# A two-layer network behind attention: the second layer in three groups of 768 tokens, its first product by seven block products, its weights decoded in batches 1 to 3

## The chip, the cores and the metric

The kernel runs on one core of a Trainium2 chip. The metric is the device time of one execution in microseconds (us), the median of three runs; lower is better. A core has TensorE (PE, matrix products into PSUM), VectorE (DVE), ScalarE (ACT), GpSimd (POOL) and SyncE (SP, which here issues every DMA, in order).

## The reference, cut to what matters

Four batches of 576 tokens (2304 in all) pass through an attention with 8 heads of 64, a gated layer, and a plain layer with SiLU:

```python
x = attention(q, k, v, s)                    # 2304 x 512
g = x @ w_gate; v = x @ w_val                # 512 -> 1536
x = (silu(g) * v) @ w_out                    # 1536 -> 512   (first layer)
h = x @ w_in                                 # 512 -> 2048
out = silu(h) @ w_out2                       # 2048 -> 512   (second layer)
```

All is float32. The weights arrive as 64-bit words and are decoded in the kernel.

## The kernel before, in words

**Products in three parts.** A matmul input is split into a rounded high part and the remainder (`hi` by an ACT copy, `lo` by a subtraction on POOL or DVE). Each product of 128 x 128 weights is three matmuls into the same PSUM bank: high x high, high x low, low x high (`mm3`, L432 to L434). Everything is held transposed: 128 features on the partitions, tokens along the free dimension.

**Decode.** A piece of weights is 512 words per partition (512 KB, tile `r64`). `decode` makes 512 float32 values of it with two ACT instructions (L392, L393) and two on DVE (L394, L397). `w_cut` then makes the high and low halves, 1024 columns at a time, on ACT (L101) and on POOL or DVE (L410).

**First layer.** Each batch runs nine chunks of 2048 weight columns, in the order of `L1`: six for gate and value, three for the way down. A chunk is 96 matmuls of 288 columns. In batch 0 its weights are decoded and also stored as float32 in DRAM (`w32`); batches 1 to 3 load them from there. While batch b runs its chunks, the attention of batch b + 1 is worked on between their steps. Batch 3 has no attention beside it. Its last chunks split the first weights of the second layer. The results go to DRAM (`x2_d`, L477).

**Second layer.** `stream` has eight chunks `uo`, each with 256 hidden features: their columns of `w_in` and their rows of `w_out2`. A chunk's weights are loaded as 64-bit words, decoded and split once. For each chunk the five token blocks of `TB` pass (four of 464 tokens, one of 448). `up2` makes two tiles of 128 hidden features with 12 matmuls each, and `silu_mul` turns them into split tiles: tanh on ACT (L441), multiply on DVE (L443), high part on ACT (L101), low part on POOL (L447). `down2` of the block before makes four output tiles with six matmuls each, and adds them into accumulators in SBUF (L525 on ACT in the first chunk, L527 on DVE after it). The split tokens (`x2_in`: load, ACT copy, DVE subtraction at L500) are made once and stay in SBUF.

**Order.** Up to the end of batch 0's attention the order of all engines is the program's. From then to the start of batch 3 PE's order is the program's and a planner with a timeline of its own orders the other engines. From batch 3 on (`manual.close()`, L644) it orders PE too. The planner may run an instruction well ahead of its place in the program where its inputs and its buffer are there. Within an engine, and within SP's DMA queue, the order is then fixed.

**Buffers.** Tiles of one tag share a fixed number of buffers in turn: five `wraw` buffers hold raw words, decoded values and loaded float32 weights; four each of `wh` and `wl` hold split weights; `ps_m` is four PSUM banks and `ps_o` four more in the second layer. A new tile waits until the earlier tile in its place is released.

## Time and profile before

| | |
|---|---|
| median of 3 runs | 1086.63 us (1085.73 to 1088.04) |
| profiled execution | 1088.26 us, span 1086.3 us |
| PE / DVE / ACT / POOL busy | 96% / 54% / 48% / 42% of the span |
| DMA | 111.90 MB, mean 103 GB/s |

The time of a run holds a little more than the span, which reaches from the first to the last recorded instruction. Busy times of different engines overlap. A matmul's recorded duration is longer than the distance to the next one, since they are pipelined; what a matmul costs is read from the distance of the starts.

### The profile page before, as it was taken

To read this page: it belongs to the slowest core of one execution; us is meant where nothing else is said; L and a number is where in the kernel's file an instruction comes from. 1 tells how busy PE (TensorE), PEld (TensorE's weight loads), DVE (VectorE), ACT (ScalarE), POOL (GpSimd) and SP (SyncE) were. 2 spreads that over 40 slices of the span, in tenths; PEclk is the share of its full clock that TensorE was granted. 3 is DMA by queue.
4 is the path that set the end of the run, shared out by engine and by line. 5 is a ranking of instruction groups with operands and counts; after the bars stand their busy time and mean duration, and the time that the engine had idled before them with its cause. 6 is when DMAs were issued, how large, how long until landed. Compare 5 with 4: busy or idle time off the path is not lost. (4 is left out here: it accounts for less than half of the span.)

```text
span 1086.3 us, 18550 instructions
## 1 busy us (share of the span) xinstructions
PE 1048.2 (96%) x6768; PEld 942.5 (87%) x6768; DVE 590.2 (54%) x1411; ACT 522.2 (48%) x1134; POOL 451.5 (42%) x587
## 2 busy tenths in 40 slices
PE   8779899999999999999989999999999999999998
PEld 5448789899998999898989999898989898898887
DVE  5668677846555646636554347615464554643333
ACT  6667776745655435655444435744243343322221
POOL 4555655554646346546315343332322232332221
PEclk8789999999999999999999999999999999999999
DMA  8556686573343334212163224601010111000012
GB/s 230 137 171 202 203 219 220 167 223 113 79 133 94 117 110 122 89 40 90 40 188 114 81 78 142 204 20 59 20 59 20 59 39 40 20 1 1 1 63 112
DMA packets 46699, 111.90 MB, mean 103 GB/s; under 512 B 7249, under 2 KB 20561, under 8 KB 46609
## 3 DMA queue, kind: packets, MB, share of 16 engines
q1 hardware_dynamic: 46608, 110.73, 33.1%
q8 instruction: 53, 0.87, 0.3%
q14 instruction: 38, 0.30, 0.1%
HBM read 91.76 MB, written 18.95 MB: 102 GB/s over the span
## 5 line engine op out<-in xcount | busy, mean ns | idle before, releaser
L447 POOL TENSOR_TENSOR h<-u,h 128x288 fp32r<-128x288 f32 (+2 forms) x176 | 195.2, 1111 | 355.8 <-ACT h L101 353.1
L432 PE MATMUL po<-h,wh 128*128 128x288 f32 (+2 forms) x704 | 233.1, 332 | 3.2 <-DVE xt L327 2.0
L432 PE MATMUL pgv<-xt,wh 128*128 128x288 f32 x768 | 229.6, 299 | 3.2 <-DVE u L443 2.0
L433 PE MATMUL po<-h,wh 128*128 128x288 f32 (+2 forms) x704 | 231.9, 329 | 0.1
L434 PE MATMUL po<-h,wl 128*128 128x288 f32 (+2 forms) x704 | 230.9, 328 | 0.0
L434 PE MATMUL pgv<-xt,wl 128*128 128x288 f32 x768 | 226.1, 294 | 0.0
L433 PE MATMUL pgv<-xt,wh 128*128 128x288 f32 x768 | 226.1, 294 | 0.0
L410 POOL TENSOR_TENSOR wl<-wraw,wh 128x1024 fp32r<-128x1024 f32 x53 | 126.6, 2390 | 158.1 <-ACT wh L101 136.1
L432 PEld LDWEIGHTS pgv<-xt,wh 128*128 128x128 f32 x768 | 144.0, 188 | 14.7 <-DVE m L218 4.5
L101 ACT ACTIVATE h<-u 128x288 fp32r<-128x288 f32 (+2 forms) x176 | 89.3, 508 | 120.4 <-DVE u L445 69.1
L432 PEld LDWEIGHTS po<-h,wh 128*128 128x128 f32 x704 | 131.9, 188 | 14.9 <-DVE m L218 2.3
L433 PEld LDWEIGHTS pgv<-xt,wh 128*128 128x128 f32 x768 | 144.2, 188 | 0.0
L434 PEld LDWEIGHTS pgv<-xt,wl 128*128 128x128 f32 x768 | 144.1, 188 | 0.0
L434 PEld LDWEIGHTS po<-h,wl 128*128 128x128 f32 x704 | 132.1, 188 | 6.9
L433 PEld LDWEIGHTS po<-h,wh 128*128 128x128 f32 x704 | 132.1, 188 | 6.8 <-POOL h L447 0.5
L443 DVE SCALAR_TENSOR_TENSOR u<-th,pu 128x464 f32<-128x464 f32 (+1 forms) x80 | 50.6, 633 | 138.3 <-ACT th L441 138.3
L527 DVE SCALAR_TENSOR_TENSOR acc<-po,acc 128x464 f32<-128x464 f32 (+1 forms) x140 | 88.4, 635 | 62.3 <-PE po L434 61.7
L101 ACT ACTIVATE wh<-wraw 128x1024 fp32r<-128x1024 f32 x88 | 92.0, 1056 | 57.6 <-PE po L433 41.8
L433 PE MATMUL pu<-x,wh 128*128 128x464 f32 (+1 forms) x320 | 118.9, 371 | 0.0
L432 PE MATMUL pu<-x,wh 128*128 128x464 f32 (+1 forms) x320 | 118.5, 370 | 0.0
L434 PE MATMUL pu<-x,wl 128*128 128x464 f32 (+1 forms) x320 | 118.5, 370 | 0.0
L231 ACT ACTIVATE e<-e,m 64x64 f32<-64x64 f32 (+4 forms) x160 | 88.6, 555 | 60.2 <-DVE m L218 59.5
(63 smaller groups left out, 1451.0 us busy)
## 6 DMA issues: line engine op xcount, KB each, us to landing
wraw<-w SPq DMA_DIRECT2D x54, 512.0 KB, 4.6
r<-in_w_dram SPq DMA_DIRECT2D x52, 512.0 KB, 6.2
qkr<-in_qk_dram SPq DMA_DIRECT2D x32, 288.0 KB, 7.4
w<-wraw SPq DMA_DIRECT2D x18, 512.0 KB, 4.0
cumb<-cum_d SPq DMA_DIRECT2D x15, 576.0 KB, 7.8
r<-in_w_dram SPq DMA_DIRECT2D x32, 256.0 KB, 3.1
x_d<-acc SPq DMA_DIRECT2D x32, 144.0 KB, 2.7
vrb<-in_vb_dram SPq DMA_DIRECT2D x16, 256.0 KB, 3.0
```

The source lines that it names most:

```text
L101: nc.scalar.activation(out=out, in_=in_, func=AF.Copy, scale=scale)
L231: nc.scalar.activation(out=e[:r, hd, :wd], in_=e[:r, hd, :wd], func=AF.Exp, bias=m[hd][:r], scale=-1.0, accum_out=l[:r, hd : hd + 1],)
L410: engines[WL[phase[c]][e]].tensor_tensor(out=wl, in0=t, in1=wh.bitcast(F32), op=ALU.subtract)
L432: nc.tensor.matmul(out=ps[:, :n], lhsT=a, rhs=xh, start=(k == 0), stop=False)
L433: nc.tensor.matmul(out=ps[:, :n], lhsT=a, rhs=xl, start=False, stop=False)
L434: nc.tensor.matmul(out=ps[:, :n], lhsT=c, rhs=xh, start=False, stop=(k == last))
L443: nc.vector.scalar_tensor_tensor(out=u, in0=th[:, :n], scalar=1.0, in1=pg[:, :n], op0=ALU.add, op1=ALU.mult)
L447: engines[LO[ph]].tensor_tensor(out=lo, in0=u, in1=hi.bitcast(F32), op=ALU.subtract)
L527: nc.vector.scalar_tensor_tensor(out=a, in0=ps[:, :n], scalar=0.5, in1=a, op0=ALU.mult, op1=ALU.add)
```

## The change

The second layer no longer takes the tokens in five blocks for every weight chunk. It runs three groups of 768 tokens (`TG`), each in two halves of 384 (`TN`), and within a group eight steps of 256 hidden features (`steps`, 24 in all).

The first product of a step is a 2 x 2 block product (halves of the 512 inputs x halves of the 256 features, against halves of the inputs x halves of the 768 tokens). It is done with seven block products in place of eight, on sums and differences of blocks (`UP`). A block product is six matmuls of 384 columns. A step's weights lie in three tiles: Z holds the three plain weight blocks that are used (768 columns), S four sums and differences of blocks, D the rows of `w_out2`. Two banks take two products each, with an ACT copy of the first one between (`s0`, `s4`); a third takes two with a copy as well (`s1`). The four results are put together on DVE and POOL, and each goes through `silu2`.

The 32 pieces of the second layer's weights are decoded in batches 1 to 3 (`ahead_load`, `ahead`) and stored as float32 in `w32`. In group 0 they are loaded, combined and split (`u_load`, `u_cut`), and the split tiles are stored in `wu_d`. Groups 1 and 2 load the split tiles. The tokens of a group are loaded and combined into seven split tiles (`x2_load`, `x2_first`, `x2_rest`), the next group's during step 7 of this one. PE keeps the program's order to the end. Split weights of the first layer now lie in one tile `wt` (high and low half).

```diff
-NCH = NGV + NO1 + NU + NO2
+NGV, NO1, NU, NO2, NPR = 6, 3, 4, 4, 8
+TG, TN = 3, 384
+UP = [("Z", 0, 0, "a"), ("S", 0, 1, "d"), ("Z", 1, 2, "a"), ("S", 1, 3, "b"), ("S", 2, 4, "c"), ("S", 3, 5, "d"), ("Z", 2, 6, "c")]
...
+    def ahead_load(i):
+        p, e = divmod(i, CW // DW)
+        t = wst["r", i] = raw_p.tile([P, DW, 2], U32, tag="wraw", name="r64")
...
+    def ahead(i):
+        p, e = divmod(i, CW // DW)
+        z = raw_p.tile([P, CW // 2], F32, tag="wraw", name="z32")
+        unpack(z[:, :DW], wst.pop(("r", i)), dec_p.tile([P, DW], U32, tag="dk", name="dk"))
+        nc.sync.dma_start(out=w32[len(L1) + p, :, e * DW : (e + 1) * DW], in_=z[:, :DW])
...
+    def x2_first(t):
+        u, d = p2["x2", 0], p2["x2", 1]
+        x2_cut(t, 0, u[:, :, 0])
+        t1 = p2["t1"] = x2_sub(t, u[:, :, 1], u[:, :, 0])
+        x2_cut(t, 1, t1)
+        x2_cut(t, 2, d[:, :, 0])
+
+    def x2_rest(t):
+        u, d = p2["x2", 0], p2["x2", 1]
+        t2 = x2_sub(t, d[:, :, 1], p2["t1"])
+        x2_cut(t, 3, t2)
+        x2_cut(t, 4, x2_sub(t, d[:, :, 1], u[:, :, 1]))
+        x2_cut(t, 5, d[:, :, 1])
+        x2_cut(t, 6, x2_sub(t, d[:, :, 0], t2))
...
+    def u_load(i):
+        t, p = steps[i]
+        for k, name in enumerate("ZSD"):
+            wide = 768 if name == "Z" else CW // 2
+            if t > 0:
+                w = p2["w", i, name] = u_tile()
+                nc.sync.dma_start(out=w[:, :, :wide].bitcast(F32), in_=wu_d[p, k, :, :, :wide])
+            elif name != "S":
+                r = p2["r", i, name] = stage(CW // 2)
...
+    def u_cut(i, names="ZSD"):
...
+                for o, a, b, op in (
+                    (s1, a21, a22, ALU.add), (s2, s1, a11, ALU.subtract),
+                    (s3, a11, a21, ALU.subtract), (s4, a12, s2, ALU.subtract),
+                ):
+                    nc.vector.tensor_tensor(out=o, in0=a, in1=b, op=op)
...
+            copy("a", hi, r[:, :wide])
+            eng = nc.vector if name == "D" else nc.gpsimd
+            eng.tensor_tensor(out=lo, in0=r[:, :wide], in1=hi.bitcast(F32), op=ALU.subtract)
+            nc.sync.dma_start(out=wu_d[p, "ZSD".index(name), :, :, :wide], in_=w[:, :, :wide].bitcast(F32))
...
+    def silu2(hi, lo, src):
+        th = p2["tmp"].tile([P, TN], F32, tag="th", name="th")
+        u = p2["tmp"].tile([P, TN], F32, tag="u", name="u")
+        nc.scalar.activation(out=th, in_=src, func=AF.Tanh, scale=0.5)
+        nc.vector.scalar_tensor_tensor(out=u, in0=th, scalar=1.0, in1=src, op0=ALU.add, op1=ALU.mult)
+        copy("a", hi, u)
+        nc.gpsimd.tensor_tensor(out=lo, in0=u, in1=hi.bitcast(F32), op=ALU.subtract)
+
+    def up2(i):
...
+        for name, k, xi, bank in UP:
+            w, x = p2["w", i, name], p2["x", t, xi]
+            fresh = bank not in ps
+            if fresh:
+                ps[bank] = ps_m.tile([P, 512], F32, tag="m", name="pu")
+            o = ps[bank][:, :TN]
+            for kk in range(2):
+                c0 = k * 256 + kk * P
+                a, c = w[:, 0, c0 : c0 + P], w[:, 1, c0 : c0 + P]
+                nc.tensor.matmul(out=o, lhsT=a, rhs=x[:, 0, kk], start=fresh and kk == 0, stop=False, skip_group_check=True)
+                nc.tensor.matmul(out=o, lhsT=a, rhs=x[:, 1, kk], start=False, stop=False, skip_group_check=True)
+                nc.tensor.matmul(out=o, lhsT=c, rhs=x[:, 0, kk], start=False, stop=kk == 1, skip_group_check=True)
+            if xi in (0, 1, 4):
+                nc.scalar.activation(out=part(f"s{xi}"), in_=o, func=AF.Copy)
+            if xi == 2:
+                silu2(h[0][0][:, 0], h[0][0][:, 1], o)
+            if xi == 3:
+                nc.vector.tensor_tensor(out=part("u2"), in0=o, in1=tmp["s0"], op=ALU.add)
+            if xi == 4:
+                nc.gpsimd.tensor_tensor(out=tmp["s1"], in0=tmp["s1"], in1=tmp["s4"], op=ALU.add)
+                nc.gpsimd.tensor_tensor(out=tmp["s1"], in0=tmp["s1"], in1=tmp["u2"], op=ALU.add)
+            if xi == 5:
+                nc.vector.tensor_tensor(out=part("c12"), in0=o, in1=tmp["u2"], op=ALU.add)
+                silu2(h[0][1][:, 0], h[0][1][:, 1], tmp["c12"])
+                silu2(h[1][1][:, 0], h[1][1][:, 1], tmp["s1"])
+            if xi == 6:
+                nc.vector.tensor_tensor(out=part("c21"), in0=o, in1=tmp["u2"], op=ALU.add)
+                silu2(h[1][0][:, 0], h[1][0][:, 1], tmp["c21"])
...
-        manual = ExitStack()
-        manual.enter_context(tc.manual_schedule(engines={mybir.EngineType.PE}))
+        everything.enter_context(tc.manual_schedule(engines={mybir.EngineType.PE}))
+        later = [[] for _ in range(n1)]
+        for i in range(NPR * CW // DW):
+            later[len(L1) + i if i < 18 else 3 * len(L1) + (i - 18) // 2].append(i)
...
-                manual.close()
+                p2["x2"] = pool("x2", 10, scope=second_layer, side="right")
...
+                if n == 0 and c == n1 - 1:
+                    u_load(0)
+                    u_cut(0)
...
+        p2["wt2"] = pool("wt2", 4, scope=second_layer)
+        p2["st"] = pool("st", 4, scope=second_layer)
+        p2["tmp"] = pool("tmp2", 1, scope=second_layer)
+        p2["h"] = pool("h2", 8, scope=second_layer)
+        u_load(1)
+        for i, (t, p) in enumerate(steps):
+            if i + 1 < len(steps):
+                u_cut(i + 1)
+            if i + 2 < len(steps):
+                u_load(i + 2)
+            if t + 1 < TG and p == 3:
+                x2_load(t + 1)
+            if t + 1 < TG and p == NPR - 1:
+                x2_first(t + 1)
+            up2(i)
+            if t + 1 < TG and p == NPR - 1:
+                x2_rest(t + 1)
+            if i > 0:
+                down2(i - 1)
+        down2(len(steps) - 1)
```

`down2(i)` is as before in kind: for each half of 384 tokens and each of four output tiles, six matmuls into a `ps_o` bank, then one instruction of 384 columns into the accumulator (ACT in step 0 of a group, DVE after it).

## Rows read from the trace of the kernel before

**Rows 1.** The page, part 1: busy us (share of the span) xinstructions.

```profile
PE 1048.2 (96%) x6768; PEld 942.5 (87%) x6768; DVE 590.2 (54%) x1411; ACT 522.2 (48%) x1134; POOL 451.5 (42%) x587
```

**Rows 2.** The page, part 4: the chain by engine, shares of the span.

```profile
PE 36%; DVE 1%; DMA 1%; issue 1%; ACT 1%; SPq 0%; DVEq 0%; ACTq 0%
```

**Rows 3.** Timeline of PE: start us, us, engine, line, operation, tile.

```profile
571.44 0.40 PE L432 MATMUL pgv<-xt,wh 128*128 128x288 f32 x1 [2.00 <-DVE u L443]
...
679.66 0.38 PE L432 MATMUL pu<-x,wh 128*128 128x464 f32 x1
```

**Rows 4.** The second layer's stretch: length, busy us by engine, PE clock, DMA share, GB/s.

```profile
679.66:1082.38 402.72, 401.40 (x1922) 359.84 (x1920) 188.22 (x283) 144.47 (x250) 114.54 (x87) 1.00 0.14 47
```

**Rows 5.** The chain in order of time: start us, us, what.

```profile
978.36 0.22 PE pu L434
...
1028.45 0.22 PE pu L434
```

**Rows 6.** Groups by form: busy us, mean ns of one, idle before.

```profile
L101 ACT ACTIVATE wh<-wraw 128x1024 fp32r<-128x1024 f32 x88 | 92.0, 1056 | 57.6 <-PE po L433 41.8 <-PE pgv L433 13.4 <-PE pu L433 1.7
...
L397 DVE SCALAR_TENSOR_TENSOR wraw<-r,dk 128x512 uint32<-128x512 uint32 x68 | 53.8, 800 | 0.6
...
L394 DVE SCALAR_TENSOR_TENSOR dk<-wraw,dk 128x512 uint32<-128x512 uint32 x68 | 50.7, 760 | 10.9 <-ACT dk L393 6.8 <-ACT wraw L392 3.7
...
L393 ACT ACTIVATE dk<-r 128x512 uint32<-128x512 uint32 x68 | 44.1, 650 | 35.4 <-DMA r<-in_w_dram 27.9 <-DVE u L443 3.0 <-DVE wraw L397 2.4
...
L392 ACT ACTIVATE wraw<-r 128x512 f32<-128x512 f32 x68 | 43.9, 667 | 21.8 <-DVE wl L410 7.6 <-DMA w<-wraw 4.8 <-issue 3.2
...
L443 DVE SCALAR_TENSOR_TENSOR u<-th,pgv 128x288 f32<-128x288 f32 x96 | 43.4, 452 | 109.3 <-ACT th L441 92.7 <-POOL h L447 11.9 <-POOL e L105 3.5
...
L443 DVE SCALAR_TENSOR_TENSOR u<-th,pu 128x464 f32<-128x464 f32 x64 | 40.7, 636 | 107.8 <-ACT th L441 107.8
...
L525 ACT ACTIVATE acc<-po 128x464 f32<-128x464 f32 x16 | 8.5, 554 | 3.6 <-PE po L434 3.6
```

**Rows 7.** A stretch at the end of layer 1, columns as in rows 4.

```profile
670.00:680.00 10.00, 10.00 (x77) 9.98 (x76) 9.29 (x17) 3.73 (x7) 2.28 (x2) 1.00 0.66 212
```

**Rows 8.** Waits of PE from 100 to 300 us: us, times, longest.

```profile
PE pv L312 <- DVE wraw L397: 6.3, 5, 3.9
```

**Rows 9.** Line L500: duration ns min/median/max, first and last start.

```profile
L500 DVE TENSOR_TENSOR x<-x2r,x x20: 611/632/646, 553.1 to 696.9; 128x464 fp32r<-128x464 f32 x16, 128x448 fp32r<-128x448 f32 x4
```

**Rows 10.** Line L410 from 575 us on, columns as in rows 9.

```profile
L410 POOL TENSOR_TENSOR wl<-wraw,wh x15: 2396/2407/2420, 577.6 to 973.2; 128x1024 fp32r<-128x1024 f32 x15
L410 DVE TENSOR_TENSOR wl<-wraw,wh x15: 1224/1980/2647, 579.1 to 988.2; 128x1024 fp32r<-128x1024 f32 x15
```

**Rows 11.** Timeline of PE and ACT, columns as in rows 3.

```profile
693.21 0.57 ACT L101 ACTIVATE h<-u 128x464 fp32r<-128x464 f32 x1
...
693.83 0.48 PE L432 MATMUL po<-h,wh 128*128 128x464 f32 x1 [1.18 <-ACT h L101]
...
1069.66 0.36 PE L434 MATMUL pu<-x,wl 128*128 128x448 f32 x1
...
1070.12 0.55 ACT L441 ACTIVATE th<-pu 128x448 f32<-128x448 f32 x1 [5.56 <-PE pu L434]
```

**Rows 12.** Timeline of POOL and DVE, columns as in rows 3.

```profile
641.16 2.41 POOL L410 TENSOR_TENSOR wl<-wraw,wh 128x1024 fp32r<-128x1024 f32 x1 [0.83 <-ACT wh L101]
...
642.67 1.99 DVE L410 TENSOR_TENSOR wl<-wraw,wh 128x1024 fp32r<-128x1024 f32 x1 [0.17 <-ACT wh L101]
...
704.62 1.20 POOL L447 TENSOR_TENSOR h<-u,h 128x464 fp32r<-128x464 f32 x1 [3.23 <-ACT h L101]
```

**Rows 13.** Two stretches with the DMA engines full, columns as in rows 4.

```profile
20.00:30.00 10.00, 9.26 (x46) 5.56 (x44) 5.42 (x20) 6.40 (x22) 6.68 (x19) 0.61 1.01 226
180.00:190.00 10.00, 10.00 (x76) 9.76 (x77) 6.69 (x25) 5.61 (x14) 6.51 (x10) 1.00 1.02 302
```

More of the change, by code (lines that the diff above doesn't have):

```diff
@@ L419, in w_split @@
                 decode(c, e)
-            for e in range(2 if stream[c] in place else 0):
+            for e in range(2):
                 w_store(c, e)
@@ new lines, with x2_load, stage, x2_cut @@
+    p2 = {}
+    def x2_load(t):
+        for i in range(2):
+            r = p2["x2", i] = p2["x2r"].tile([P, 2, 2, TN], F32, tag="x2r", name="x2r")
+            src = x2_d[2 * i : 2 * i + 2, :, 2 * t * TN : 2 * (t + 1) * TN]
+            nc.sync.dma_start(out=r, in_=src.rearrange("k p (h n) -> p k h n", h=2))
+    def stage(n):
+        return p2["st"].tile([P, CW // 2], F32, tag="wraw", name="stage")[:, :n]
+    def x2_cut(t, i, src):
+        x = p2["x", t, i] = p2["x2"].tile([P, 2, 2, TN], F32R, tag="x2", name="x2")
+        copy("a", x[:, 0], src)
+        nc.vector.tensor_tensor(out=x[:, 1], in0=src, in1=x[:, 0].bitcast(F32), op=ALU.subtract)
@@ new lines, in down2 @@
+    def down2(i):
+        t, p = steps[i]
+        h, w = hs.pop(("2", i)), p2["w", i, "D"]
+        for n in range(2):
+            for m in range(KD):
+                ps = p2["ps"].tile([P, 512], F32, tag="o", name="po2")[:, :TN]
+                for f in range(2):
+                    c0 = f * 512 + m * P
+                    a, c = w[:, 0, c0 : c0 + P], w[:, 1, c0 : c0 + P]
+                    hi, lo = h[f][n][:, 0], h[f][n][:, 1]
+                    nc.tensor.matmul(out=ps, lhsT=a, rhs=hi, start=f == 0, stop=False)
+                    nc.tensor.matmul(out=ps, lhsT=a, rhs=lo, start=False, stop=False)
+                    nc.tensor.matmul(out=ps, lhsT=c, rhs=hi, start=False, stop=f == 1)
+                if p == 0:
+                    accs["2", m, n] = p2["acc"].tile([P, TN], F32, tag=f"acc_{m}_{n}", name="acc2")
+                a = accs["2", m, n]
+                if p == 0:
+                    nc.scalar.activation(out=a, in_=ps, func=AF.Copy, scale=0.5)
+                else:
+                    nc.vector.scalar_tensor_tensor(out=a, in0=ps, scalar=0.5, in1=a, op0=ALU.mult, op1=ALU.add)
+                if p == NPR - 1:
+                    t0 = (2 * t + n) * TN
+                    nc.sync.dma_start(out=out[m * P : (m + 1) * P, t0 : t0 + TN], in_=a)
@@ L532 @@
+    steps = [(t, p) for t in range(TG) for p in range(NPR)]
     units = [(b, g, half) for b in range(B) for g in range(NP) for half in "AB"]
@@ L666, in body @@
                     w_ahead(c)
+                    for i in later[c]:
+                        ahead(i)
+                    for i in later[c + 1] if c + 1 < n1 else []:
+                        ahead_load(i)
+                if n == 0 and c == n1 - 1:
+                    u_load(0)
+                    u_cut(0)
                 if n * 4 % len(cur) == 0:
```

166 lines of the change are left out of this document (72 added, 94 removed).

## The prediction

> **What bounds the kernel now.** I read the page first, then the chain, then the stretches, then single forms. TensorE (PE) is busy for 96% of the span [rows 1]. The chain that ended last is 36% PE and next to nothing else [rows 2]; it reaches back some 40% of the span, so the whole second layer hangs on PE. [...] So only fewer or shorter matmuls shorten this layer, and every wait that is added to PE lengthens it.
>
> Two prices come from the rows of time [rows 3, 5]. One weight chunk of the second layer (240 matmuls, four token blocks of 464 and one of 448) recurs after 1028.45 - 978.36 = 50.09 us, or 208.7 ns a matmul at 460.8 columns on average. Eight such are 400.7, so about 2 us of the 402.7 were a wait at its start. In layer 1, 816 matmuls of 288 columns (batch 3's nine chunks of 96, less the 48 issued before) stand between 571.44 and 679.66: 132.6 ns each. That is 0.440 ns for a column between the two sizes.
>
> **The change, part by part.**
>
> *Matmuls.* Before, 40 blocks of 48 are 1920. After, 24 steps of 7 x 6 = 42 (first product) and 48 (second product) are 2160, all of 384 columns. At 132.6 + 96 x 0.440 = 174.9 ns a step takes 15.74 us and the layer 377.8. Columns fall by 6.25%, but 240 more matmuls pay their fixed part, so the gain is less than that share. Against 402.7: **-24.9 us**. [...]
>
> *Decode in batches 1 to 3.* 32 pieces are added there, each with two ACT instructions (667 + 650 ns) and two on VectorE (DVE: 760 + 800 ns) [rows 6], a 512 KB load, and a 256 KB store that waits in SP's in-order queue. They leave the second layer, where they cost PE nothing. Two stretches tell what they cost beside layer 1. Where the last chunks of layer 1 already carried decodes (670 to 680), DVE was 9.29 of 10 us busy and PE never stopped [rows 7]. Where 100 to 300 us carried four pieces a chunk beside attention, PE waited 6.3 us in all for the last decode step [rows 8]. Batches 1 and 2 get one piece a chunk, batch 3 two without attention. Between 0 and 7; I take **+2**, near the first row since the density is half or a quarter. Five buffers now serve six tiles a chunk in batch 3, so a weight load can wait for the preceding decode; a chunk of 96 matmuls is 12.7 us and the load is wanted one chunk later, which hides it.
>
> *PE's order* in batch 3 and layer 2 becomes the program's own. There are four PSUM banks and no reordering around a late operand any more. The waits that matter are priced next.
>
> *Start of layer 2.* Token tiles come from batches 0 and 1 and can be made early: before, the first such cut (L500) ran at 553.1 us, long ahead of its place in the program [rows 9]. Step 0's weights use layer 1's buffers; the S tile of step 1 can't be made before layer 1's last matmul frees them. Four subtractions of 256 columns on DVE (0.41 each, between rows of 464 and 1024 columns), an ACT copy (1.06) and a POOL subtraction (2.41) [rows 6, 10] make 5.1 us plus queueing, against 7.35 + 1.05 = 8.4 us until it is wanted. 0 to 6, I take **+2**; the old 2 us are already out of the 377.8.
>
> *The copies inside the first product.* Bank a is copied by ACT after its first product (s0) and then gets a second one; bank c likewise (s4). One other product, 6 x 0.1749 = 1.05 us, stands between. From the start of a product's last matmul to ACT's start took 0.46 us (1069.66 to 1070.12), and from the end of an ACT instruction (693.21 + 0.57) to PE's start 0.05 [rows 11]; a 384-column copy is about 0.49 by the 464-column one of 554 ns [rows 6]. That is 1.00 of the 1.22 us until PE wants it, less some 0.2 for loading weights ahead: just in time if ACT is free. ACT is free at s0 in groups 1 and 2; in group 0 its weight copies (1.06 for 1024 columns) can stand in the way. Of 48 such places I charge the 16 of group 0 with 0.15 us and the other 32 with 0.05: **+4**, between 0 and 12 (0.25 each).
>
> *DVE and POOL in group 0.* Each step of group 0 also makes weights. On DVE alone: S 4 x 0.41, the D remainder 1.22, 15 instructions of 384 columns at 0.55 (between 452 and 636 ns [rows 6]): 11.2 us. On POOL: 768 columns 1.86, 1024 columns 2.41, six of 384 at 1.03 (from 1.20 at 464 columns and 2.41 at 1024 [rows 12]): 10.4 us. Both fit into 15.74 by themselves. But the trace shows them in each other's way: the same DVE subtraction of 1024 columns took 1.224 to 2.647 us [rows 10], and the one that began at 642.67, inside a POOL subtraction that ended at 643.57, ended at 644.66, 1.09 us after POOL's, which is its time alone [rows 12]. So it waited for POOL to finish. Eight DVE instructions of a step read two operands in SBUF (4 S, D, three of the silu). Were each to wait half of a mean POOL instruction (10.4 / 8 / 2 = 0.65 us), DVE would need 16.4 us, 0.7 over the step: **+5** for eight steps. None: 0. A whole POOL instruction each time (1.30): 21.6, or 5.9 x 8 = +47. I take the half, as a DVE instruction that collides does so at an arbitrary point. DVE's accumulations have four banks, so about 3 us of lateness reach PE only after that.
>
> [...]
>
> *Group changes.* Seven token tiles are cut and four differences formed, 11 DVE instructions of 768 columns at 0.95: 10.5 us. Ten buffers let three be made early; the other four wait for products of the last step. DVE then has 8.3 (15 x 0.55) + 4 cuts and 3 subtractions (6.7) + some 2 of collisions = 17 of the 15.74 + 3.1 us until the fourth product wants them. **+2** for two changes (0 to 6).
>
> *Transfers.* A group-0 step loads 1.05 MB and stores 2.88, 3.93 MB in 15.74 us: 250 GB/s. Where the engines were saturated they moved 226 (share 1.01) and 302 GB/s (1.02) [rows 13]. At 302 it fits: **0**. At 226 a step takes 17.4: +1.65 x 8 = +13. I take the first, since it too moved 512 KB loads with stores between. Groups 1 and 2 load 2.88 MB a step, 183 GB/s, less than either.
>
> *End.* The last product's accumulation and store are alike: 0 (0.3 either way).
>
> **Sum.** -24.9 + 2 + 2 + 4 + 5 + 2 = -9.9 against the profiled execution, whose span is 1086.3 and whose time is 1088.26. That gives 1078.4. It lay 1.6 above the median of the runs shown (1086.63), so on that scale **1077**.
>
> **Rivals.**
>
> *DVE and POOL set the pace of group 0, and it ends slower.* Place: the eight weight-making steps. For it: eight instructions on each side, POOL 10.4 of 15.74 us busy, and a row that shows one waiting out the other. Against: PE tolerates a late accumulation by some 3 us, and the order in the queues may keep them apart. Each step then costs 11.2 + 8 x wait. With waits of 0.98 us (midway between half and whole) a step is 19.0 us, +26 instead of +5: 1098. It turns slower from a wait of about 0.85 us (18.0, +18, which with the rest gives 1090), and the whole range of it is 1086 to 1119.
>
> *Nearly everything hides.* No copy is late, collisions stay within DVE's reserve, decode costs nothing: -24.9 + 3, about 1065. For it: PE waited only some 2 us in the whole second layer of before, with the same silu chain. Against: the copies' tight 0.2 us.
>
> *Transfers bind group 0.* At 226 GB/s: 1077 + 13 = 1090. For it: 3.93 MB a step, more than any longer stretch of before moved. Against: large rows, and the windows at 302.
>
> *The matmuls don't get cheaper.* If the spacing at 384 columns were not on the line between 288 and 464, the gain would be gone at 400.7 / 2160 = 185.5 ns; both neighbours make that improbable and I count it within the first rival's chance.
>
> **How the numbers follow.** Forecast (1066 to 1084, likeliest 1077) 0.55; pair-bound group 0 0.20; all hidden 0.18; transfers 0.07. A measurement of this kernel tells about 0.2% (2.2 us) from none: faster is below 1084.5. Faster 0.52 + 0.17 = 0.69; same 0.09 (edges of the forecast and the milder rivals); slower 0.22. The range runs from 1064 (nearly all hidden) to 1094, which holds the transfers' case and the milder half of the pair's.
>
> **What would show it.** Steps of 15.7 us in groups 1 and 2, with matmuls 175 ns apart on average; a layer start near 682; PE waits for ACT copies at the third and last product of a step, most in group 0; DVE subtractions of 1024 columns near 2 us there; steps of 16 to 17 us in group 0. I am wrong if group 0's steps take 18 us or more, if PE waits for weights or transfers, or if layer 1 ends more than 7 us later.

## The result and the profile after

The changed kernel takes **1102.47 us** (median of 4 runs, 1100.17 to 1105.68), the kernel before 1087.1 on the same chip: ratio 1.0145, 95% interval 1.011 to 1.0179. It is slower; 1077 was predicted, with a range to 1094. Its profiled execution took 1104.66 us with a span of 1102.9.

First the page of the changed kernel, parts 1 and 4 (columns as in [rows 1, 2]):

```profile
PE 1040.6 (94%) x7008; PEld 968.5 (88%) x7008; DVE 672.6 (61%) x1572; ACT 567.1 (51%) x1251; POOL 521.5 (47%) x659
...
PE 31%; DVE 6%; DMA 4%; issue 3%; ACT 3%; POOL 1%; SPq 0%; DVEq 0%; ACTq 0%
```

PE is busy for less time than before, 1040.6 against 1048.2 us [rows 1], in a longer span. So the time went into waits, and the chain, which was nearly PE alone [rows 2], now runs through DVE, DMA and ACT too. Where, the starts of three PE instructions tell: the first product of layer 2, its first down product, and its seventh (columns as in [rows 3]):

```profile
699.74 0.34 PE L598 MATMUL pu<-x,wt 128*128 128x384 f32 x1
...
728.76 0.52 PE L628 MATMUL po<-h,wt 128*128 128x384 f32 x1
...
829.75 0.34 PE L628 MATMUL po<-h,wt 128*128 128x384 f32 x1
```

- Layer 1 ends at 699.74, not 679.66 [rows 3]: **+20.1 us**. Against before, chunk by chunk, the kernel is 2.5 ahead at 217 us, loses 6.3 in batch 0's last chunk and 2.2 in batches 1 and 2, gains 5.0 back where batch 3 begins, and loses 19.1 from batch 3's second chunk to its end (11.6 of it up to 667 us, 6.2 in the chunk from there).
- From there to the seventh down product are 130.0 us. Its 8 x 42 + 6 x 48 = 624 matmuls need 109.1 at 174.9 ns: **20.9 lost**. The first two products alone take 29.0 instead of 14.7.
- The rest, to the last matmul, takes 269.3 us, and 269.3 to 269.6 in every kernel with this matmul schedule.

Four stretches of the changed kernel, columns as in [rows 4]:

```profile
670.00:680.00 10.00, 7.25 (x37) 6.62 (x36) 10.00 (x14) 3.50 (x6) 1.89 (x1) 0.74 0.72 246
710.00:720.00 10.00, 9.15 (x36) 8.83 (x36) 7.03 (x8) 3.85 (x6) 8.94 (x7) 0.71 0.99 371
720.00:730.00 10.00, 5.24 (x18) 5.24 (x19) 7.28 (x6) 4.04 (x9) 7.74 (x6) 0.66 0.95 351
949.20:1074.00 124.80, 124.80 (x715) 124.71 (x715) 63.77 (x115) 49.35 (x100) 48.43 (x48) 1.00 0.49 175
```

The last one is the new schedule at its best: 124.80 / 715 = 174.5 ns a matmul, no gap. The first is [rows 7]'s stretch: 77 matmuls then, 37 now. The two in the middle hold the start of layer 2, at a granted clock of 0.71 and 0.66.

**What stopped layer 1.** PE's longest waits from 565 to 670 us (columns as in [rows 8]):

```profile
PE pgv L438 <- DVE u L447: 5.3, 6, 1.2
PE po L438 <- DVE u L447: 1.6, 2, 0.9
PE po L438 <- DVE acc L478: 0.9, 1, 0.9
```

One of them in the timeline of ACT, DVE and PE:

```profile
654.36 0.67 ACT L366 ACTIVATE dk<-r 128x512 uint32<-128x512 uint32 x1 [2.44 <-DMA r<-in_w_dram]
...
654.93 0.40 ACT L445 ACTIVATE th<-pgv 128x288 f32<-128x288 f32 x1
...
655.43 0.46 DVE L447 SCALAR_TENSOR_TENSOR u<-th,pgv 128x288 f32<-128x288 f32 x1 [3.99 <-ACT th L445]
...
655.94 0.40 PE L438 MATMUL po<-h,wt 128*128 128x288 f32 x1 [0.88 <-DVE u L447]
```

Read it from the bottom. PE wants the bank that the multiply L447 still reads; that waits for the tanh L445; and the tanh stands on ACT behind a decode instruction (L366) that sat 2.44 us until its words had landed. In batch 0's last chunk the same happens at full size:

```profile
231.24 0.66 ACT L366 ACTIVATE dk<-r 128x512 uint32<-128x512 uint32 x1 [8.13 <-DMA r<-in_w_dram]
231.80 0.39 ACT L445 ACTIVATE th<-pgv 128x288 f32<-128x288 f32 x1
...
232.81 1.33 PE L312 MATMUL pv<-pt,vz 128*64 128x320 f32 x4 [3.78 <-DVE u L447]
```

PE's last matmul ahead of this stop ended at 229.02, so the tanh's products were there by then. Yet in ACT's 8.13 us of idleness it does not run: it starts only behind the decode, at 231.80.

The chunk from 667 us on takes 18.9 us instead of 12.7, and there it is another queue: seven cuts of the second layer's tokens (L508) stand on DVE between layer 1's own instructions from 667 to 679 us, and one of them, beside a POOL subtraction of 3.04 us, took 2.79 where the next took 0.94. DVE is busy for 10.00 of 10 us (the first stretch above). POOL, DVE and PE:

```profile
668.86 3.04 POOL L416 TENSOR_TENSOR wt<-wraw,wt 128x1024 fp32r<-128x1024 f32 x1 [8.30 <-issue]
...
669.92 2.79 DVE L508 TENSOR_TENSOR x<-stage,x 128x768 fp32r<-128x768 f32 x1
...
674.00 0.41 PE L438 MATMUL pgv<-xt,wt 128*128 128x288 f32 x1 [2.08 <-DVE acc L478]
```

**What stopped layer 2.** PE stops twice in the first two products. The first stop, 3.60 us, is ahead of step 0's last product, which wants the copy s4. On ACT that copy stood behind cuts of step 1's weights, which waited for a load and for DVE's sums:

```profile
704.84 0.85 ACT L100 ACTIVATE wt<-stage 128x768 fp32r<-128x768 f32 x1 [2.29 <-DMA stage<-w]
...
707.96 1.06 ACT L100 ACTIVATE wt<-stage 128x1024 fp32r<-128x1024 f32 x1 [0.33 <-DVE stage L560]
...
709.86 0.69 PE L598 MATMUL pu<-x,wt 128*128 128x384 f32 x1 [3.60 <-ACT s L602]
```

For the second, PE's longest wait, first four rows of DVE and POOL, then the chain into it:

```profile
712.66 3.92 DVE L560 TENSOR_TENSOR stage<-stage 128x256 f32<-128x256 f32 x3
...
714.29 2.01 POOL L568 TENSOR_TENSOR wt<-stage,wt 128x768 fp32r<-128x768 f32 x1
...
717.78 0.42 DVE L560 TENSOR_TENSOR stage<-stage 128x256 f32<-128x256 f32 x1
...
719.47 2.35 POOL L568 TENSOR_TENSOR wt<-stage,wt 128x1024 fp32r<-128x1024 f32 x1
...
720.35 2.54 DVE L568 TENSOR_TENSOR wt<-stage,wt 128x1024 fp32r<-128x1024 f32 x1 [1.56 <-ACT wt L100]
...
722.82 0.55 DVE L575 SCALAR_TENSOR_TENSOR u<-th,s 128x384 f32<-128x384 f32 x1
...
723.39 0.52 ACT L100 ACTIVATE h<-u 128x384 fp32r<-128x384 f32 x1 [2.29 <-DVE u L575]
...
724.24 0.47 ACT L602 ACTIVATE s<-pu 128x384 f32<-128x384 f32 x1
...
724.76 0.69 PE L598 MATMUL pu<-x,wt 128*128 128x384 f32 x1 [5.61 <-ACT s L602]
```

Three sums of 256 columns took 3.92 us (the lone one at 717.78: 0.42). The 1024-column subtraction took 2.54, not 1.22 [rows 10]: it ended at 722.89, 1.07 us after the POOL instruction beside it (719.47 + 2.35 = 721.82). Behind it stood a silu step, behind that on ACT the rounding and a tanh, and behind those the copy that PE wants. It is s1: PE has issued 72 of the first two steps' 84 matmuls, and the next product, the sixth of step 1, goes into the bank that s1 is copied from. The pool of s1 has one buffer (`pool("tmp2", 1)`), and the silu step at 722.82 is the last to read step 0's s1, so this copy could not come before 723.37. The matmuls then ran at clock 0.66 to 0.71: 54 of them were busy for 9.15 + 5.24 us from 710 to 730, where 54 x 0.1749 = 9.45 would do, so 4.9 us went there beside the waits.

### The profile page after: what moved, and what is told of

It reads as the page before. It is cut to its first block, busy times and chain, and to the rows that moved or that the text cites. A ratio compares the mean times of both kernels' runs of the same rounds, so it can differ in the third digit from the quotient of the medians.

```text
span 1102.9 us, 19660 instructions
## 1 busy us (share of the span) xinstructions
PE 1040.6 (94%) x7008; PEld 968.5 (88%) x7008; DVE 672.6 (61%) x1572; ACT 567.1 (51%) x1251; POOL 521.5 (47%) x659
## 5 line engine op out<-in xcount | busy, mean ns | idle before, releaser
L438 PE MATMUL pgv<-xt,wt 128*128 128x288 f32 x768 | 232.0, 302 | 9.7 <-DVE u L447 6.0
L439 PE MATMUL pgv<-xt,wt 128*128 128x288 f32 x768 | 227.5, 296 | 0.0
L440 PE MATMUL pgv<-xt,wt 128*128 128x288 f32 x768 | 227.5, 296 | 0.0
L577 POOL TENSOR_TENSOR h<-u,h 128x384 fp32r<-128x384 f32 x96 | 102.4, 1067 | 192.8 <-ACT h L100 192.8
L416 POOL TENSOR_TENSOR wt<-wraw,wt 128x1024 fp32r<-128x1024 f32 x45 | 107.9, 2398 | 143.0 <-ACT wt L100 111.2
L100 ACT ACTIVATE h<-u 128x288 fp32r<-128x288 f32 (+1 forms) x192 | 92.2, 481 | 157.1 <-DVE u L575 108.2
L438 PEld LDWEIGHTS pgv<-xt,wt 128*128 128x128 f32 x768 | 145.4, 189 | 23.5 <-DVE u L447 7.7
L439 PEld LDWEIGHTS pgv<-xt,wt 128*128 128x128 f32 x768 | 145.5, 189 | 0.0
L440 PEld LDWEIGHTS pgv<-xt,wt 128*128 128x128 f32 x768 | 145.3, 189 | 0.0
L628 PE MATMUL po<-h,wt 128*128 128x384 f32 x384 | 129.6, 338 | 2.2 <-DVE acc L637 2.2
L450 POOL TENSOR_TENSOR h<-u,h 128x288 fp32r<-128x288 f32 x96 | 93.6, 978 | 79.0 <-ACT h L100 77.7
L629 PE MATMUL po<-h,wt 128*128 128x384 f32 x384 | 128.6, 335 | 0.0
L630 PE MATMUL po<-h,wt 128*128 128x384 f32 x384 | 128.4, 334 | 0.0
L598 PE MATMUL pu<-x,wt 128*128 128x384 f32 x336 | 116.4, 346 | 10.8 <-ACT s L602 10.8
L438 PE MATMUL po<-h,wt 128*128 128x288 f32 x384 | 115.3, 300 | 2.7 <-DVE u L447 1.6
L600 PE MATMUL pu<-x,wt 128*128 128x384 f32 x336 | 115.6, 344 | 0.0
L599 PE MATMUL pu<-x,wt 128*128 128x384 f32 x336 | 115.6, 344 | 0.0
L439 PE MATMUL po<-h,wt 128*128 128x288 f32 x384 | 113.2, 295 | 1.0 <-POOL h L450 1.0
L440 PE MATMUL po<-h,wt 128*128 128x288 f32 x384 | 113.0, 294 | 0.0
L637 DVE SCALAR_TENSOR_TENSOR acc<-po,acc 128x384 f32<-128x384 f32 x168 | 91.4, 553 | 34.0 <-PE po L630 33.4
L447 DVE SCALAR_TENSOR_TENSOR u<-th,pgv 128x288 f32<-128x288 f32 x96 | 43.2, 450 | 89.3 <-ACT th L445 81.0
```

The source lines that it names most:

```text
L100: nc.scalar.activation(out=out, in_=in_, func=AF.Copy, scale=scale)
L416: engines[WL[phase[c]][e]].tensor_tensor(out=wl, in0=t, in1=wh.bitcast(F32), op=ALU.subtract)
L438: nc.tensor.matmul(out=ps[:, :n], lhsT=a, rhs=xh, start=(k == 0), stop=False)
L439: nc.tensor.matmul(out=ps[:, :n], lhsT=a, rhs=xl, start=False, stop=False)
L440: nc.tensor.matmul(out=ps[:, :n], lhsT=c, rhs=xh, start=False, stop=(k == last))
L598: nc.tensor.matmul(out=o, lhsT=a, rhs=x[:, 0, kk], start=fresh and kk == 0, stop=False, skip_group_check=True)
```

## The experiments

Two questions. *Layer 1*: do decode instructions that wait for their loads at the head of ACT's queue hold it up, or is it PE's fixed order in batch 3? *Layer 2's group 0*: do DVE and POOL hold each other up (the prediction's first rival), or is it the order of the queues at the start, or the transfers? The letters in an expectation stand for the theories that it describes. "Stretch" is from layer 1's end to the seventh down product.

| run | median us | ratio to the kernel before, 95% interval | layer 1 ends | first two products | stretch |
|---|---|---|---|---|---|
| after | 1102.47 | 1.011 to 1.0179 | 699.7 | 29.0 | 130.0 |
| e1_no_ahead | 1077.38 | 0.9889 to 0.994 | 671.9 | 28.8 | 129.6 |
| e2_decode_b12 | 1109.52 | 1.0185 to 1.0223 | 705.4 | 29.0 | 129.9 |
| e4_stage_kept | 1100.96 | 1.0102 to 1.0151 | 698.4 | 26.6 | 127.1 |
| e6_planner_b3 | 1105.34 | 1.014 to 1.0195 | 697.8 | 29.0 | 133.4 |
| e5b_sharedz | 1100.81 | 1.0103 to 1.0136 | 698.4 | 28.7 | 131.9 |
| e5_hold | 1083.91 | 0.9953 to 0.9977 | 678.5 | 28.4 | 129.8 |
| e7_trans | 1103.82 | 1.0136 to 1.0166 | 698.2 | 16.5 | 129.8 |
| e8_both | 1082.73 | 0.9943 to 0.9973 | 680.6 | 16.5 | 129.7 |
| e10_nostore | 1085.81 | 0.9968 to 0.9993 | 680.0 | 31.6 | 132.2 |
| e9_actlo | 1076.53 | 0.9875 to 0.9914 | 675.8 | 25.1 | 123.7 |
| e11_sdec | 1074.91 | 0.9863 to 0.9899 | 676.3 | 22.5 | 124.2 |
| e14_sdec_actlo | 1073.33 | 0.9861 to 0.9892 | 677.4 | 23.5 | 121.1 |
| e12_sdec_trans | 1070.32 | 0.9833 to 0.9872 | 674.2 | 15.5 | 119.2 |
| e16_lopool | 1079.44 | 0.9906 to 0.9945 | 677.8 | 15.3 | 127.9 |
| e15_lodve | **1064.73** | 0.9777 to 0.9812 | 677.3 | 15.5 | 112.5 |
| e17_lodve1 | 1098.55 | 1.0076 to 1.0125 | 699.6 | 22.7 | 124.2 |

The planner orders the other engines anew in every kernel. Five that leave layer 2's program as it is (e1, e2, e5b, e5, e6) have a stretch of 129.6 to 133.4 us and first two products of 28.4 to 29.0, so a difference of 2 or 3 us in the stretch alone shows little.

**e1: no decode in batches 1 to 3.** This leaves the decode out; group 0 reads other weights, as many bytes.

```diff
-            later[len(L1) + i if i < 18 else 3 * len(L1) + (i - 18) // 2].append(i)
+            pass
```

> Leaves out the decode of the second layer's weights in batches 1 to 3 (32 pieces with loads and stores); group 0 reads the first layer's decoded weights instead, so transfers and work there stay. Theory A (an ACT decode instruction that waits for its load holds up the tanh queued behind it, and PE then runs out of free PSUM banks): the PE waits at 233 us (3.8) and the ten between 580 and 661 us (about 9 with their restarts) go, layer 1 ends at 684 to 688 us in place of 699.7, and the time falls by 11 to 16 us from 1102 to about 1089; the stop at 671 to 682 us and the 14 us at the layer's start stay. Rival B (PE's order in batch 3, now the program's, costs the time): less than 3 us change.

Layer 1 ends 27.8 us earlier, with no wait of PE left in batch 3; the stretch is unchanged. That is more than theory A gave, and more than the loss of 20.1: against the kernel before, e1 is ahead by 2.8 us at 217 us and by another 4.9 where batch 3 begins. So the decodes cost layer 1 27.8 us, and gains of 7.7 from elsewhere, whose cause was not tried, hid part of it. The stop at 670 us, which the expectation took for something apart, went too: without decodes the seven token cuts ran from 627 to 646 us, and every chunk of batch 3 takes 12.7 us. Layer 2's loss is another matter.

**e2: all 32 pieces in batches 1 and 2.**

```diff
+            later[len(L1) + i * 18 // 32].append(i)
```

> All 32 pieces decoded in batches 1 and 2, none in batch 3. Theory A: batch 3 loses its ten waits (about 9 us), batches 1 and 2 gain a few (their ACT waits for loads were up to 5.4 us and cost PE nothing beside 233 us): 3 to 8 us less, about 1097. Rival B: no change beyond 2 us.

Both theories missed this: a gain of 3 to 8 us or no change was expected, and it is 7.1 slower. Batch 3 runs clean, but the two batches lose 27.6 us instead of 2.2, and layer 1 ends later still. ACT's waits in them, from 240 to 395 and from 395 to 565 us, first of the changed kernel, then of this one:

```profile
ACT dk L366 <- DMA r<-in_w_dram: 16.5, 8, 5.4
...
ACT dk L366 <- DMA r<-in_w_dram: 24.4, 11, 4.1
```

```profile
ACT dk L366 <- DMA r<-in_w_dram: 26.6, 13, 4.3
...
ACT dk L366 <- DMA r<-in_w_dram: 37.2, 15, 3.9
```

With one piece a chunk most of these waits meet no one who is in need; with nearly two more of them do. PE's own waits there are 7.8 us for L447, as in batch 3, and 9.4 for an instruction of the attention on DVE (L218). That the second kind goes back to the same wait on ACT was not tried. Batches 1 and 2 are at any rate no free place for decodes.

**e4: the start's raw buffers kept, step 1's load in layer 1's last chunk.**

```diff
+    raw_p = pool("raw", 5)
...
+                    u_load(1)
...
-        p2["st"] = pool("st", 4, scope=second_layer)
```

> The five raw buffers stay for the second layer's stages and step 1's raw weights are loaded during layer 1's last chunk, so that ACT's weight copies for step 1 no longer wait for loads ahead of the copies of the first product. Theory A (queue order on ACT behind a late load): the first two up-products take 17 to 20 us in place of 29.0, time 9 to 12 us less, about 1092; the granted clock stays at 1.00 there. Rival C (transfers saturated at 305 to 371 GB/s at 700 to 730 us set the pace): at most 3 us less.

The first two products take 26.6 us, where 17 to 20 were expected, 2.4 less than before: the late load is a small part of it.

**e6: the planner orders PE in batch 3 again,** and the program does from layer 2 on.

```diff
+        manual = ExitStack()
+        manual.enter_context(tc.manual_schedule(engines={mybir.EngineType.PE}))
...
+                manual.close()
```

> The planner orders PE in batch 3 again, as before; the second layer keeps the program's order. Rival B (the fixed order of PE costs layer 1's time): batch 3 loses most of its 13 to 14 us, about 1090. Theory A: PE's instructions are ready in the same order, within 4 us of 1102.

Nothing is gained: layer 1 ends 1.9 us earlier and the stretch takes 3.4 longer. PE's order is not the cause.

**e5b and e5.** Two pieces of batch 3 share one buffer (e5b); e5 also takes each decode from the planner and puts it behind the last ACT instruction of a quarter chunk, with its load issued half a chunk ahead.

```diff
+        if not two or i % 2 == 0:
+            p2["z"] = raw_p.tile([P, CW // 2], F32, tag="wraw", name="z32")
```

```diff
+                if n * 4 % len(cur) == 0 and n * 4 // len(cur) in (1, 2):
+                    for i in later[c][n * 4 // len(cur) - 1 :: 2]:
+                        ins = next(x for x in reversed(nc.cur_bb.bb.instructions) if x.engine == mybir.EngineType.Activation)
+                        with tc.issue_after(ins):
+                            ahead(i)
+                    if n * 4 // len(cur) == 2:
+                        for i in later[c + 1] if c + 1 < n1 else []:
+                            ahead_load(i)
```

> Only the buffers of the run before it: two pieces of batch 3 share one buffer, so a load there no longer waits for the next chunk's split; the queue order is left to the planner. Theory A: some of the late loads of batch 3 come earlier, but the planner also puts the decodes earlier: 0 to 5 us less, about 1100. If it gains as much as the held version, the buffers were the cause and not the queue order.

> All the decode work stays in batches 1 to 3, but each piece's ACT instructions are queued behind the ACT instructions of the chunk's second or third quarter, its load is issued half a chunk to a chunk ahead, and in batch 3 two pieces share one buffer, so that no decode waits for its load at the head of ACT's queue. Theory A (it is the wait at the head of the queue, not the work): layer 1 ends at 676 to 688 us in place of 699.7, PE's waits for DVE u in batch 3 fall from 9 to under 3 us, time 1102 - 14 = about 1088 (within 5). Rival D (it is the decode's work on ACT and DVE, 42 and 50 us, that collides with the layer's own): layer 1 ends at 694 or later, time 1096 or more.

The buffer alone does nothing that can be told (1.7 us). With the place and the time of the load, which were changed together, it is 18.6 us. ACT's waits for words from 565 to 672 us, of the changed kernel and of e5:

```profile
ACT dk L366 <- DMA r<-in_w_dram: 18.5, 8, 4.9
```

```profile
ACT z L365 <- DMA r<-in_w_dram: 1.7, 1, 1.7
```

All the decode work is still there, and layer 1 ends 21.2 us earlier. So 21.2 of the 27.8 us that e1 showed are not the work but where it stood in the queue; the other 6.6 stay with the work or with the waits that are left. (Kernels with this edit end layer 1 between 674.2 and 680.6, so a few us there say little.)

**e7 and e8: another order at the start.** Z and S of steps 0 and 1 are cut in layer 1's last chunk, D and step 2's cuts are put behind the copy s4, and the silu has two buffers. e8 is e5 and e7 together. The copies s0, s1 and s4 keep one buffer each.

```diff
+                    u_cut(0, "ZS")
+                    u_load(1)
+                    u_cut(1, "ZS")
...
+            if i == 1:
+                with tc.issue_after(p2["s4"]):
+                    u_cut(1, "D")
+                u_load(2)
+                with tc.issue_after(p2["s4"]):
+                    u_cut(2)
```

> Only the start of layer 2: raw buffers kept, Z and S of steps 0 and 1 cut in layer 1's last chunk or directly at its end, the weight cuts of D and of step 2 queued on ACT behind the copies of steps 0 and 1, two buffers for the silu's tiles. Theory A (queue order at the start, then the lower clock that follows the stop): the first two up-products take 15 to 19 us in place of 29.0, the clock stays at 1.00, time about 1102 - 11 = 1091. Rival D (the work of weights, DVE and POOL in each other's way, sets the start's pace): 24 us or more, time 1097 or more.

> Both of the above together. Theory A: the gains add up, 1102 - 14 - 11 = about 1077 (1070 to 1084), faster than the kernel before. Rival D: 1092 or more.

The first two products fall to 16.5 us, as theory A expected, yet the stretch stays at 129.8 and the time at 1103.8, not 1091: the stop only moved to step 2, which then took 24.2. e8 lies in its range through e5's part alone; e7's adds 1.2 us. An order can move such a loss while the work behind it is unchanged.

**e10: e5 without the stores of the split weights.** These are left out.

```diff
-            nc.sync.dma_start(out=wu_d[p, "ZSD".index(name), :, :, :wide], in_=w[:, :, :wide].bitcast(F32))
```

> The held version without the stores of split weights in group 0 (left out; groups 1 and 2 load the float32 weights' bytes in their place, as many bytes as before). 2.9 of group 0's 3.9 MB a step go. Rival C (transfers at 300 to 420 GB/s set the pace of group 0's start): group 0's first part falls from 130 to 120 us or less, time 1074 or less. Theory D: 127 to 131 us, time 1081 to 1085.

The transfers are not it: the DMA engines' share of the stretch falls from 0.71 to 0.27, and the stretch takes 132.2 us, no less than 129.8.

**e9 and e11: less for DVE and POOL to do.** e9 is e5 with the low halves of Z and S as ACT copies, which leaves the subtraction out. e11 is e5 with S's four sums made once, where the pieces are decoded, and loaded in group 0; nothing is left out of it.

```diff
+                copy("a", lo, r[:, :wide])
```

```diff
+            if e == 1:
+                r = raw_p.tile([P, CW // 2], F32, tag="wraw", name="s32")
+                s_sums(z, r)
+                nc.sync.dma_start(out=ws_d[p], in_=r)
```

> The held version (1083.9) with the low halves of Z and S written by an ACT copy in place of POOL's subtraction (left out: that subtraction, so the second layer's products are wrong). It takes 4.3 us of two-operand work a step off POOL and adds 1.9 to ACT. Theory D (DVE and POOL in each other's way set the pace of group 0, from its start on): from layer 1's end to the seventh down-product 112 to 118 us in place of 130, time about 1084 - 14 = 1070. Theory A alone (order and late loads on ACT): ACT is fuller, so 128 us or more, time 1082 or more. Rival C (transfers): no change, 1084.

> The held version with the four sums of S made once at the decode in batches 1 and 2 and stored, so that group 0 loads them (512 KB a step more, 1.65 us of DVE's two-operand work a step less there); complete computation. Theory D: group 0's first part 118 to 124 us in place of 130, layer 1 at most 2 us longer, time about 1084 - 8 = 1076. Rival C: more transfers, 130 us or more, 1084 or more.

They take 6.1 and 5.6 us off the stretch. e9's 123.7 lies between its forecasts (112 to 118, or 128 and more), e11's 124.2 just outside the theory's 118 to 124: the mechanism has the right sign, but less of the loss than was expected. e11 is 1.2% faster than the kernel before, with everything computed; e5 was at 0.35%.

**e12 and e14: what is left.** e12 is e11 with e7's start; e14 is e11 with e9's copies, again without the subtraction.

> e11 with the reordered start of e7: layer 1's raw buffers are kept, Z and S of steps 0 and 1 are cut in layer 1's last chunk, D and step 2's cuts are held behind the s4 copy, the silu has two buffers. Theory D (the DVE and POOL work that makes weights paces the eight steps of group 0, and a better order only moves the stop, as in e7): first two products near 16 us, but the stretch to the seventh down product 120 to 124 us as in e11 (124.2), time 1072 to 1076. Rival Q (with S's sums gone, what is left at the start is queue order): first two products 15 to 17 us, the stretch 113 to 118, time 1065 to 1070.

> e11 with the low halves of Z and S made by an ACT copy in place of the POOL subtraction (this leaves the remainder out). Takes the last large POOL instructions off the eight steps and adds two ACT copies of about 1 us to a step. Theory D: as e9 did beside e5 (-6 us), the stretch to the seventh down product falls from 124.2 to 116 to 120, time 1067 to 1072. Rival Q: what is left is ACT's and SP's queue order at the start, so more ACT work there makes it no shorter: the stretch 123 to 127, time 1074 to 1078.

Both come out between their two forecasts, with 5.0 and 3.0 us off the stretch: with less work in the way the order counts too (e12). e12 shows what is left, in one collision (POOL, DVE, PE) and the stretch behind it:

```profile
760.83 2.68 POOL L578 TENSOR_TENSOR wt<-stage,wt 128x1024 fp32r<-128x1024 f32 x1
...
761.67 2.92 DVE L578 TENSOR_TENSOR wt<-stage,wt 128x1024 fp32r<-128x1024 f32 x1
...
765.12 0.44 PE L639 MATMUL po<-h,wt 128*128 128x384 f32 x1 [1.99 <-DVE acc L648]
```

```profile
765.00:770.00 5.00, 4.88 (x18) 4.61 (x19) 4.32 (x8) 1.05 (x2) 2.46 (x3) 0.66 0.95 393
```

DVE's subtraction ends at 764.59, 1.08 us after POOL's at 763.51; the accumulation that frees PE's bank stands behind it; and the granted clock is 0.66 from 765 to 770 us, after the stop. Which DVE instructions suffer, the silu's multiply shows: one line, one shape, with its source `pu` in PSUM or `s` and `c` in SBUF (columns as in [rows 9], 674 to 800 us of e12):

```profile
L585 DVE SCALAR_TENSOR_TENSOR u<-th,c x15: 542/796/2008, 682.8 to 797.3; 128x384 f32<-128x384 f32 x15
L585 DVE SCALAR_TENSOR_TENSOR u<-th,pu x8: 540/551/555, 678.1 to 790.4; 128x384 f32<-128x384 f32 x8
L585 DVE SCALAR_TENSOR_TENSOR u<-th,s x8: 560/1044/2749, 683.9 to 798.7; 128x384 f32<-128x384 f32 x8
```

With one operand in PSUM it never takes over 0.555 us; with both in SBUF up to 2.749. Only 3 of the 8 with `pu` began while a POOL instruction ran, so the accumulations, which have one operand in PSUM, are the better check: 21 of these 40 did (the stretch of e12, with at least 0.25 us of POOL's to come), and none was longer than 0.558:

```profile
L648 DVE SCALAR_TENSOR_TENSOR acc<-po,acc x40: 540/545/558, 711.2 to 786.1; 128x384 f32<-128x384 f32 x40
```

Of the multiplies with `s` and `c` in the same stretch, the 13 that began so took 1.46 us in the mean, the other 8 0.55. So in these rows the instructions that take longer beside POOL are those with both operands in SBUF; what holds them up there was not shown.

**e15, e16, e17: who subtracts.** If POOL's long instructions are the cause, giving DVE *more* work and POOL none of the long ones must help. e15 does that to e12, e16 the opposite, e17 the same to the changed kernel itself.

```diff
-            eng = nc.vector if name == "D" else nc.gpsimd
+            eng = nc.vector
```

```diff
-            eng = nc.vector if name == "D" else nc.gpsimd
+            eng = nc.gpsimd
```

> e12 with the low halves of Z and S subtracted on DVE in place of POOL; nothing is left out. DVE gets 2.2 us more work in a step (about 9.5 + 2.2 = 11.7 us), POOL loses its two long instructions (10.4 - 4.3 = 6.1 us). Theory L (DVE's two-operand instructions stand still while a long POOL instruction runs): the stretch from layer 1's end to the seventh down product falls from 119.2 to 111 to 116, time 1062 to 1067. Rival W (DVE's amount of work and its queue are the limit): it grows to 121 to 126, time 1072 to 1077.

> e12 with D's low half subtracted on POOL in place of DVE; nothing is left out. DVE loses its 1024-column instruction of each step (about 8.3 us left), POOL gets a third long one (10.4 + 2.4 = 12.8 us). Theory L: more of a step is under a long POOL instruction, and DVE's small two-operand instructions (silu) meet it: the stretch 119 to 125, time 1070 to 1076. Rival W: 113 to 117, time 1064 to 1068.

> The changed kernel with one word different: the low halves of Z and S are subtracted on DVE in place of POOL; nothing is left out. Layer 1's end stays near 698 to 700. DVE's work in a step of group 0 becomes 11.2 + 2.2 = 13.4 us. Theory L (DVE stands still under POOL's long subtractions): the stretch to the seventh down product falls from 130 to 116 to 123, time 1088 to 1096. Rival W (DVE's amount of work and its queue): 130 to 136, time 1103 to 1109.

e15 lands where theory L put it: 112.5 us, 3.4 above the bare matmuls, 1064.73 us. The same multiply and the stretch, in e15:

```profile
L585 DVE SCALAR_TENSOR_TENSOR u<-th,c x16: 544/819/1366, 685.9 to 797.2; 128x384 f32<-128x384 f32 x16
L585 DVE SCALAR_TENSOR_TENSOR u<-th,s x8: 543/547/1210, 687.0 to 795.1; 128x384 f32<-128x384 f32 x8
```

```profile
677.30:789.76 112.46, 110.40 (x626) 109.03 (x625) 87.84 (x125) 66.50 (x120) 51.12 (x44) 1.00 0.80 311
```

With `c` the multiply is still stretched, to 1.37 us at most instead of 2.01: POOL keeps its 384-column instructions. One rival is not held apart: e15 also empties POOL's own queue, in which the silu's low halves stand. In e12's stretch PE waited 3.4 us for DVE, 3.0 for ACT and never for POOL; DVE waited 4.0 us for POOL, and 2.2 in e15. So that queue can hardly be most of the 6.7 us between them, but no run holds it fixed.

e16 is worse than either theory said; its largest wait is for POOL's own queue, the silu's low half behind three long instructions:

```profile
PE po L640 <- POOL h L587: 7.4, 1, 7.4
```

e17 gains 5.8 us of the stretch, between the two forecasts (124.2 where 116 to 123 or 130 to 136 were expected): in the changed kernel DVE still makes the sums there, and the start's order is as it was. So the long subtractions are about a quarter of its loss in group 0 by themselves; the sums and the order, taken with them, make up most of the rest, as e11, e12 and e15 show one after the other; 3.4 us stay in e15.

## Why the prediction was wrong

*Matmuls*: right. 174.5 ns against 174.9, and 269.3 us for the part after the seventh down product, where the sum without any wait has 377.8 - 109.1 = 268.7. Copies and group changes there cost 0.6 us together, less than the parts of +4 and +2 that fell to it.

*Decode in batches 1 to 3, "+2 (0 to 7)"*: the step that failed most. Layer 1 ends **+20.1** later, and the decodes alone cost 27.8 (e1). The prediction counted the work (four instructions, one load, one store) and found room for it on every engine. The room was there: e5 holds all of it and ends layer 1 at 678.5. What it did not ask was what stands behind the first decode instruction while its load is under way; the one wait it did weigh ("a weight load can wait for the preceding decode") was of another kind. The token cuts ("can be made early"), which run from 667 us with the decodes and from 627 without, were put at nothing too. [rows 6] held a hint that was not used: ACT was idle for 27.9 us ahead of L393, ended by `DMA r<-in_w_dram`, in the kernel before. [rows 7 and 8] were taken as prices for the density of work, but they come from stretches with other places in the queues.

*PE's order*: right that it is no cost of its own (e6).

*Start of layer 2, "+2 (0 to 6)"*: **+14.3** (29.0 less 14.7), 9.2 of it in two waits for ACT's copies and 4.9 at the granted clock of 0.66 to 0.71. The prediction priced step 1's S tile alone, 5.1 us against 8.4 until it is wanted. The queueing that it named and gave no size was the matter: the loads of that step were issued behind stores of layer 1 at 699.96, and the weights of two steps and the tokens' cuts then met on ACT, DVE and POOL within 20 us. Of the copies it priced s0 and s4. The longest wait, 5.61 us, was for s1, which has three products' time instead of one but stood behind a multiply that was itself late.

*DVE and POOL in group 0, "+5 (0 to 47)", and the copies, 2.4 of "+4"*: the steps from the first to the seventh down product take 101.0 us where six of 15.74 are 94.4, **+6.6**; the size is right, the reason only in part. The prediction let a collision cost PE something only where DVE's sum exceeds the step. The rows of DVE, 700 to 830 us of the changed kernel (columns as in [rows 6]), and that stretch from the first to the seventh:

```profile
L560 DVE TENSOR_TENSOR stage<-stage 128x256 f32<-128x256 f32 x28 | 19.8, 735 | 3.3 <-DMA stage<-w 3.3
L568 DVE TENSOR_TENSOR wt<-stage,wt 128x1024 fp32r<-128x1024 f32 x8 | 18.9, 2363 | 3.3 <-ACT wt L100 3.3
```

```profile
699.74:829.76 130.02, 117.67 (x627) 113.34 (x626) 97.42 (x139) 65.63 (x120) 82.13 (x58) 0.95 0.71 257
```

These two forms were stretched by 28 x (735 - 410) + 8 x (2363 - 1220) = 18.2 us, 2.3 a step where the prediction had 8 x 0.65 = 5.2 for all. (That the eight with both operands in SBUF are the ones that wait was assumed there; in e12 such multiplies took up to 2.749 us, and the accumulations 0.558 at most.) DVE was busy only 97.4 of 130.0 us. So DVE did not lack throughput; a stretched instruction made the next one late, that made ACT's copy late, and PE, with its four banks and fixed order, had no other work. The "about 3 us of lateness" that banks absorb does not hold for s0 and s4, which PE needs within 1.05 us, nor did it suffice for s1. The start and these steps are one loss, as e7 shows: with the start in order it came back in step 2. The first rival's mechanism was the right one, at a place where the forecast did not look for it. (The prediction's "1.09 us after POOL's, which is its time alone" is 0.13 short of the 1.22 in [rows 10]; no sum hangs on it.) A stop then cost more than itself: at the start the granted clock was 1.00 from 699.74 to 706 us, before the first stop, 0.71 and 0.66 in the 20 us from 710 on, where 4.9 us went beside the waits, and 1.00 again from 730 to 740. e15 gains by giving the busier engine more to do, which a sum of work can't explain.

*Transfers, "0"*: right (e10).

The sum, to the last matmul's start: layer 1 +20.1; layer 2 from 402.3 to 399.3, -3.0, where -24.9 + 2 + 4 + 5 + 2 = -11.9 was forecast. With +2 for the decodes that was -9.9; it is +17.1.

Of the signs it had set for being wrong one appeared: layer 1 ended 20.1 us later, more than 7. Group 0's steps behind the start took 16.8 us on average, not 18, and PE's recorded waits there were for ACT's copies and DVE's accumulations, not for weights or transfers. "Nearly everything hides, about 1065" was a fair price for the change when the queues are in order: e15 has 1064.73. In part that is luck, since e15 ends layer 1 2.4 us earlier than before, which no term named, and loses 3.4 in the stretch.

What stays open: the 6.3 us in batch 0's last chunk were not tried alone (e1 and e5 remove them with the rest); what gained 2.8 us in batch 0 and 4.9 where batch 3 begins (e6 has the second gain too, so PE's order is not it); whether a second buffer for s1 would have spared the longest wait in the changed kernel; and of e16's queue on POOL only the one wait was read.

## What to carry to other kernels

Work that "fits" on an engine still costs if its first instruction waits for a transfer at the head of an in-order queue (21.2 of 27.8 us here): ask what stands behind it, issue the load early, and put the instruction behind the urgent ones. Price a late instruction by the chain that it delays, not by the engine's busy share; where PE can't reorder, every link to it must be on time, and a stop was paid again in clock here (4.9 us at 0.66 to 0.71). Before giving two-operand work to POOL to relieve DVE, see whether DVE's instructions with both operands in SBUF take longer beside it (the silu's multiply in e12: up to 2.749 us, and 0.555 at most with one operand in PSUM); the kernel with more work on DVE can be the faster one (e15, 1064.73 us, against e12, 1070.32).

## What the runs showed of the hardware that was not expected

- POOL's instructions are stretched as well as DVE's: its 1024-column subtraction took 3.13 us at the longest and 2.65 in the mean from 700 to 830 us of the changed kernel, 2.41 before [rows 10].
- Full DMA engines did not tell the rate here: at a share of 1.01 to 1.02, 226 and 302 GB/s were the rates in [rows 13], and in e12

```profile
710.00:720.00 10.00, 10.00 (x59) 10.00 (x58) 7.66 (x12) 5.30 (x9) 8.63 (x6) 1.00 1.02 417
720.00:730.00 10.00, 10.00 (x59) 10.00 (x58) 6.26 (x9) 5.03 (x9) 8.33 (x6) 1.00 1.02 419
```

with PE never idle. The rival that took 226 GB/s as a limit had no ground.
